# Attention and wave MLP on one core: batches woven in pairs in a fixed order, with x transposed by the DMA crossbar from SBUF to SBUF

## The chip, the cores and the metric

One NeuronCore of a Trainium2 chip. The metric is the time of one execution on the device in microseconds (us); a profile of one execution comes with each kernel. Its span, from the first to the last instruction, is shorter than the time of the same execution: by 1.7 to 2.0 us in every run of which both are on record.

## The reference

Two phases over batch 8, 8 heads, 576 tokens, head size 64 (model width 512). Inputs and output are float32.

```python
# attention in chunks of 64 tokens
scores = q_c @ k_c.T / sqrt(64)            # per head and chunk
x = softmax(scores) @ v_c                  # -> [8, 576, 512]
# wave MLP
theta = x @ w_theta
zr, zi = x * cos(theta), x * sin(theta)
y = w_tok_r @ zr + w_tok_i @ zi            # over the 576 tokens of a batch
u = x + y
out = u + max(u @ w_ch, 0)
```

## The kernel before

It runs attention for all eight batches, keeping x in SBUF, then the MLP for all eight. Tokens lie in five blocks per batch: four of 128 and one of 64. Products are in fp16 with fp32 sums. The MLP, where x has to be transposed for theta and u for the last product:

```python
for b in range(B):
    for sb in range(NSB):                            # five token blocks
        for db in range(NDB):                        # four blocks of 128 channels
            nc.tensor.transpose(pxt[:, db, 0:ns], x16[b][...], id16[0:ns, 0:ns])
        nc.scalar.copy(out=xT[:, :, sb*P : sb*P+ns], in_=pxt[:, :, 0:ns])
    for sb in range(NSB):
        for db in range(NDB):                        # theta: 128 x 512 products
            nc.tensor.matmul(pth[0:ns], xT[:, db, sb*P : sb*P+ns], wtheta16[:, db, :], ...)
        # ScalarE: cos16, sin16;  VectorE: zr16 = x*cos, zi16 = x*sin
    for mt in range(NSB):                            # y: 10 products per block
        ... nc.tensor.matmul(psy[0:nt], wT[0:ns, sb, tsl], z[0:ns, sb, :], ...)
        # VectorE: u16 = psy + x16
    # u16 transposed on TensorE, copied by ScalarE (as x above), then u @ w_ch,
    # VectorE: o32 = max(puw, 0) + u16, and a store on SyncE's queue
    ... (cut)
```

The softmax here doesn't subtract the row's maximum and nothing guards it: scores larger than these inputs give would overflow.

## Time and profile before

| | before |
|---|---|
| time, median of 2 runs | 332.54 us (331.72 to 333.35) |
| span | 329.0 us |
| TensorE busy | 285.2 us, 87% |
| VectorE / ScalarE / GpSimd busy | 44% / 35% / 32% |
| attention, 27 to 127 us | granted clock 0.65 |
| MLP, 127 to 329 us | granted clock 0.97 to 0.99; one batch 24.12 us, all of it TensorE |

The busy shares are averages over two stages with different limits; the lines that show this are in the prediction below. "Granted clock" is the share of TensorE's full clock that the throttle allowed in a stretch.

### The profile page before, as it was taken

To read this page: it belongs to the slowest core of one execution; us is meant where nothing else is said; L and a number is where in the kernel's file an instruction comes from. 1 tells how busy PE (TensorE), PEld (TensorE's weight loads), DVE (VectorE), ACT (ScalarE), POOL (GpSimd) and SP (SyncE) were. 2 spreads that over 40 slices of the span, in tenths; PEclk is the share of its full clock that TensorE was granted. 3 is DMA by queue.
4 is the path that set the end of the run, shared out by engine and by line. 5 is a ranking of instruction groups with operands and counts; after the bars stand their busy time and mean duration, and the time that the engine had idled before them with its cause. 6 is when DMAs were issued, how large, how long until landed. Compare 5 with 4: busy or idle time off the path is not lost.

```text
span 329.0 us, 7260 instructions
## 1 busy us (share of the span) xinstructions
PE 285.2 (87%) x3138; PEld 159.2 (48%) x3138; DVE 146.2 (44%) x319; ACT 115.7 (35%) x290; POOL 105.4 (32%) x132
## 2 busy tenths in 40 slices
PE   0328977879869889999999999999999999999992
PEld 0216866768858777334344344344344344344340
DVE  0216437357347354544534625525535534533532
ACT  0001440431421424805615515425426326227220
POOL 8189999999999900000000000000000000000000
PEclk9999577575676576999999999999999999999998
DMA  6999999999999980003003004004004003003004
GB/s 107 175 134 152 146 138 138 149 142 140 151 138 144 147 44 3 2 0 130 16 0 131 16 0 140 5 0 145 0 0 146 0 0 131 14 1 129 15 1 144
DMA packets 120064, 26.44 MB, mean 80 GB/s; under 512 B 113248, under 2 KB 115424, under 8 KB 120032
## 3 DMA queue, kind: packets, MB, share of 16 engines
q0 software_dynamic: 114784, 16.54, 79.4%
q1 hardware_dynamic: 5248, 9.44, 8.4%
q8 instruction: 24, 0.39, 0.5%
q14 instruction: 8, 0.07, 0.1%
HBM read 33.06 MB, written 9.44 MB: 129 GB/s over the span
## 4 chain that ended last, share of the span: by engine, by line
PE 62%; POOL 14%; DMA 12%; DVE 7%; issue 2%; ACT 1%; DVEq 0%; POOLq 0%; ACTq 0%
PE ps_y L251 30%; POOL qk L107 9%; PE ps_theta L219 8%; PE ps_uw L282 8%; DMA out_dram<-o 5%; POOL v L107 5%; DMA wtok_nat<-in_moe_w_tok_r_dram 3%; PE ps_uT L269 3%; PE ps_sT L142 3%; PE ps_xT L202 2%; PE ps_rs L161 2%; PE ps_wtokT L78 2%; DVE o L290 2%; DMA wtok_nat<-in_moe_w_tok_i_dram 2%; DMA qk<-in_q_dram 2%
## 5 line engine op out<-in xcount | busy, mean ns | idle before, releaser
L251 PE MATMUL ps_y<-zr,wtokTr 128*128 128x512 f16 (+3 forms) x200 | 53.9, 382 | 0.7 <-DVE zr L234 0.6
L251 PE MATMUL ps_y<-zi,wtokTi 128*128 128x512 f16 (+3 forms) x200 | 54.5, 384 | 0.0
L259 DVE TENSOR_TENSOR u<-ps_y,x 128x512 f16<-128x512 f32 (+1 forms) x40 | 27.6, 690 | 53.6 <-PE ps_y L251 53.6
L147 ACT ACTIVATE eT<-ps_sT 128x256 f16<-128x256 f32 x64 | 24.4, 382 | 69.5 <-PE ps_sT L142 66.7
L274 ACT COPY uT<-ps_uT 128x512 f16<-128x512 f16 (+1 forms) x40 | 18.6, 564 | 82.3 <-PE ps_uT L269 82.3
L290 DVE SCALAR_TENSOR_TENSOR o<-ps_uw,u 128x512 f32<-128x512 f32 (+1 forms) x40 | 27.6, 690 | 40.0 <-DMA out_dram<-o 22.5
L107 POOL DMA_DIRECT2D v<-in_v_dram x40 | 37.3, 933 | 1.5 <-DMA wch<-in_moe_w_ch_dram 1.3
L107 POOL DMA_DIRECT2D qk<-in_q_dram x40 | 37.3, 933 | 1.2 <-issue 0.8
L219 PE MATMUL ps_theta<-wtheta,xT 128*128 128x512 f16 (+1 forms) x160 | 36.9, 381 | 0.7 <-ACT xT L207 0.7
L107 POOL DMA_DIRECT2D qk<-in_k_dram x40 | 37.3, 932 | 0.1
L282 PE MATMUL ps_uw<-wch,uT 128*128 128x512 f16 (+1 forms) x160 | 36.9, 381 | 0.0
L251 PEld LDWEIGHTS <-wtokTi 128*128 128x128 f16 (+3 forms) x200 | 16.5, 99 | 38.5 <-issue 29.3
L120 PE MATMUL ps_qkT<-id,qk 128*128 128x128 f16 (+1 forms) x320 | 29.9, 267 | 5.8 <-DMA qk<-in_q_dram 4.5
L142 PE MATMUL ps_sT<-qT,kT 64*64 64x64 f16 x576 | 30.1, 232 | 3.7 <-DVE kT L130 3.6
L251 PEld LDWEIGHTS <-wtokTr 128*128 128x128 f16 (+3 forms) x200 | 17.8, 99 | 31.9 <-issue 17.0
L161 PE MATMUL ps_rs<-ones,eT 64*64 64x1 f16 x576 | 26.9, 191 | 7.0 <-ACT eT L147 7.0
L120 PEld LDWEIGHTS <-qk 128*128 128x128 f16 (+1 forms) x320 | 26.1, 127 | 8.7 <-DMA qk<-in_q_dram 6.1
L230 ACT ACTIVATE sin<-ps_theta,zerob 128x512 f16<-128x512 f32 (+1 forms) x40 | 29.6, 741 | 0.0
L226 ACT ACTIVATE cos<-ps_theta,pihalf 128x512 f16<-128x512 f32 (+1 forms) x40 | 29.5, 737 | 0.0
L207 ACT COPY xT<-ps_xT 128x512 f16<-128x512 f16 (+1 forms) x40 | 18.6, 564 | 28.2 <-PE ps_xT L202 28.2
L161 PEld LDWEIGHTS <-eT 64*64 64x64 f16 x576 | 21.8, 144 | 11.1 <-ACT eT L147 8.9
L185 DVE TENSOR_TENSOR x<-ps_xout,recip 128x512 f16<-128x512 f32 (+1 forms) x40 | 24.6, 681 | 0.4
(39 smaller groups left out, 242.2 us busy)
## 6 DMA issues: line engine op xcount, KB each, us to landing
out_dram<-o SPq DMA_DIRECT2D x32, 256.0 KB, 2.0
qk<-in_q_dram POOLq DMA_DIRECT2D x32, 128.0 KB, 5.5
qk<-in_k_dram POOLq DMA_DIRECT2D x32, 128.0 KB, 5.8
v<-in_v_dram POOLq DMA_DIRECT2D x32, 128.0 KB, 5.8
out_dram<-o SPq DMA_DIRECT2D x8, 128.0 KB, 2.3
wtok_nat<-in_moe_w_tok_r_dram POOLq DMA_DIRECT2D x1, 576.0 KB, 10.0
wtok_nat<-in_moe_w_tok_i_dram POOLq DMA_DIRECT2D x1, 576.0 KB, 6.1
wtheta<-in_moe_w_theta_dram POOLq DMA_DIRECT2D x1, 512.0 KB, 6.1
```

The costliest lines, as they stand in the source:

```text
L107: nc.gpsimd.dma_start(dst, t_ap[b, :, sb * P : sb * P + ns, :].rearrange("h s d -> s h d"),)
L120: nc.tensor.transpose(pqk[:, which, e, 0:ns], qk16[0:ns, sb, which, 2 * e : 2 * e + 2, :].rearrange("s h d -> s (h d)"), id16[0:ns, 0:ns],)
L142: nc.tensor.matmul(pst[cp * CH : cp * CH + CH, cb, :], kT[par * D : par * D + D, e, sl], qT[par * D : par * D + D, e, sl],)
L161: nc.tensor.matmul(ps_rs[cp * CH : cp * CH + CH, cb, h : h + 1], eT[cp * CH : cp * CH + CH, h, cb, :], ones16[cp * CH : cp * CH + CH, :],)
L185: nc.vector.tensor_tensor(out=x16[b][0:ns, sb, :].rearrange("s (h d) -> s h d", h=H), in0=psx[0:ns], in1=recip[0:ns, sb, :].unsqueeze(-1). ...
L219: nc.tensor.matmul(pth[0:ns], xT[:, db, sb * P : sb * P + ns], wtheta16[:, db, :], start=(db == 0), stop=(db == NDB - 1),)
L226: nc.scalar.activation(out=cos16[0:ns, sb, :], in_=pth[0:ns], func=AF.Sin, bias=pihalf[0:ns], scale=1.0,)
L230: nc.scalar.activation(out=sin16[0:ns, sb, :], in_=pth[0:ns], func=AF.Sin, bias=zerob[0:ns], scale=1.0,)
L251: nc.tensor.matmul(psy[0:nt], wT[0:ns, sb, tsl], z[0:ns, sb, :], start=(step == 0), stop=(step == nsteps - 1),)
L259: nc.vector.tensor_tensor(out=u16[0:nt, mt, :], in0=psy[0:nt], in1=x16[b][0:nt, mt, :], op=ALU.add,)
L282: nc.tensor.matmul(puw[0:nt], uT[:, db, mt * P : mt * P + nt], wch16[:, db, :], start=(db == 0), stop=(db == NDB - 1),)
L290: nc.vector.scalar_tensor_tensor(out=o32[0:nt], in0=puw[0:nt], scalar=0.0, in1=u16[0:nt, mt, :], op0=ALU.max, op1=ALU.add,)
```

## The change

The intent: the two stages bind different things, so run them woven. Two batches become one pair of 1152 tokens, nine full tiles of 128 instead of ten blocks. While TensorE does the MLP of pair p, steps of attention of pair p+1 are put between its steps, in an order that the program fixes. y comes out already transposed, row sums come from a column of ones in v, and x is transposed not by TensorE and ScalarE but by a DMA through the crossbar, SBUF to SBUF, issued from SyncE's queue, where the output stores and two small moves of the middle tile stand too. The diff, cut to its core:

```diff
+def weave(main, filler):                 # spread the filler steps evenly over the main steps
+    ...
+    def a1(p, g): ...                    # q, k transposed on TensorE, copied by VectorE
+    def a2(p, g): ...                    # scores, exp
+    def a3(p, j, g): ...                 # numerator and row sum, x tile j (VectorE)
+    def a4(p, g):
+        j0, n = GROUPS[g]                # groups of 2, 2, 1, 2, 2 tiles
+        for j in range(j0, j0 + n):
+            nc.sync.dma_start_transpose(
+                st[p]["xT"][:, :, j * P : j * P + P], st[p]["x"][:, j, :]
+            )
+    def a5(p, g): ...                    # theta from xT, cos, sin, zr, zi
+    def y(p, bb, db): ...                # y transposed: 9 x 2 products of 288 columns
+    def w(p, j): ...                     # u @ w_ch, u back by identity, relu, sum, store (SyncE)
+    def back(p, gs):
+        steps = []
+        for i in range(len(gs) + 2):
+            if i < len(gs):
+                j0, n = GROUPS[gs[i]]
+                steps += [c(a3, p, j, gs[i]) for j in range(j0, j0 + n)]
+            if 0 <= i - 1 < len(gs):
+                steps.append(c(a4, p, gs[i - 1]))     # one group after its x
+            if 0 <= i - 2 < len(gs):
+                steps.append(c(a5, p, gs[i - 2]))     # two groups after its x
+        return steps
+    # pair 0:        weave(y0, rest of its own attention), weave(y1, front(1)), weave(w, back(1))
+    # pairs 1 and 2: weave(y0, front(p+1)), weave(y1 and w, back(p+1))
+    # pair 3:        y0, y1 and w alone
-    for b in range(B): ...               # the attention loop and the MLP loop go
```

## The prediction

> **What bounds the kernel now.** I read the page's slices first, then the windows of its stages, then the chain that ended last in order of time, then the groups of instructions by shape.
>
> ```profile
> PE   0328977879869889999999999999999999999992
> PEclk9999577575676576999999999999999999999998
> DMA  6999999999999980003003004004004003003004
> 27.00:127.20 100.20, 83.68 (x2050) 74.48 (x2050) 51.95 (x136) 30.20 (x128) 87.27 (x105) 0.65 2.25 130
> 152.97:329.00 176.03, 169.12 (x910) 69.60 (x910) 78.05 (x143) 72.47 (x140) 0.00 (x0) 0.99 0.15 51
> ```
>
> Two programs run one after the other. Until 127 us (15 slices) the DMA engines are full and TensorE's granted clock is 0.65 on average: attention of eight batches, 100.2/8 = 12.5 us each, after 27 us in which TensorE hardly works. Then loads are over, the clock is 0.99, TensorE is busy without a gap: the MLP. (Columns of the windows: stretch, length, busy us of PE, weight loads, DVE, ACT, POOL, then clock, DMA share, GB/s.)
>
> ```profile
> 201.15 1.22 PE ps_xT L202 x20
> 202.37 4.54 PE ps_theta L219 x20
> 206.91 12.60 PE ps_y L251 x50
> 219.51 1.22 PE ps_uT L269 x20
> 220.73 4.54 PE ps_uw L282 x20
> ```
>
> This is one batch of the MLP in the chain (start, us, what): nothing but TensorE, 1.22 + 4.54 + 12.60 + 1.22 + 4.54 = 24.12 us, eight times. So in this stage a column taken from TensorE is worth its time, and work of ACT and DVE is free.
>
> ```profile
> 62.27 0.88 POOL v L107
> 63.14 1.37 POOL qk L107 x2
> L180 PE MATMUL ps_xout<-v,eT 64*64 64x64 f16 x576 | 23.3, 238 | 0.0
> L120 PE MATMUL ps_qkT<-id,qk 128*128 128x128 f16 x256 | 25.2, 285 | 0.8 <-DMA qk<-in_k_dram 0.8
> ```
>
> In attention, up to 88 us, the chain is mostly GpSimd issuing q, k and v loads, one per 0.87 us for 128 tokens and 0.67 for 64. The 285 ns of a transpose is its pipelined duration; its spacing is 1.22/20 = 61 ns in the MLP stage and 2.71/32 = 85 ns under the low clock. The 64x64 products come every 1.93/61 = 32 ns.
>
> **What the Trainium skill says.** "TensorE: Matmul & The Clock Gate", Back-to-back issue gap: N/2.4 + 2.5 ns when warm, 216 ns for N = 512. The trace agrees: 20 theta products are 20 x 0.2158 = 4.32 us, and the remaining 0.22 of 4.54 is a bubble at the change to the 64-column group. I use the formula for N = 288: 122.5 ns, an estimate. The same page, The HAM clock gate: activity releases a throttle to half clock; the trace agrees in kind (0.65 among small products, 0.99 among large ones). "VectorE: DVE Perf Modes", The three transpose paths: 1309 ns for a 128x128 DMA crossbar transpose, 390 on TensorE; no run yet shows the first. "Advanced Engine Details and Errata", X-Bar Transpose (TRN2): transposes as fast as regular DMAs. From these I estimate 2 to 4 us from issue to landing of one 128x512 transpose; the 256 KB output stores of this trace land in 2.0.
>
> **The change part by part.** Two batches become one sequence of 1152 tokens, nine full tiles of 128 instead of 2 x (4 full + 1 half). TensorE per pair, at full clock:
>
> - q/k transposes: 9 x 8 = 72 x 61 ns = 4.4 us.
> - Scores: 9 x 16 = 144 x 32 ns = 4.6. Numerator: also 144, 4.6. The row sums (2 x 72 products) go: a column of ones in v gives them (65 columns for 64).
> - x transposes leave TensorE (2 x 1.22 = 2.4 saved) and their ten copies (0.56 us each) leave ACT.
> - theta: 9 x 4 = 36 x 216 ns = 7.8 (before 2 x 4.54 = 9.1).
> - y: 2 x 4 x 9 x 2 = 144 products of 288 columns x 122.5 ns = 17.6 (before 25.2). Fully used K blocks (nine per batch, real and imaginary tails sharing one, instead of ten) and 576 = 2 x 288 columns do this; y comes out transposed, so the u transposes go.
> - w: 36 x (216 + 61) = 10.0, the 61 being the product with the identity that brings u back (before 2 x (4.54 + 1.22) = 11.5).
>
> Sum: 49.0 us per pair. Before, a pair took 2 x (12.5 + 24.1) = 73.2. The new program changes between small and large products some 14 times each way per pair; at half the 0.22 us bubble above per edge that is 3 us, and I allow 2 more for a clock below full where attention is woven in: 54 per pair.
>
> The other engines, per pair, from the durations of before (about 1.1 ns a column for ACT, 0.62 us for 512 fp32 columns and 0.34 for 512 fp16 ones on DVE): ACT exp 5.0, cosine and sine 10.0, relu 5.2, two or three table loads of 1.28, about 23; DVE 5.2 (q/k copies) + 6.5 (x) + 5.4 (z) + 5.6 (u) + 5.6 (out) = 28. Loads: 24 x 0.87 + 6 x 0.67 = 25 us of issuing. All are under 54, so TensorE should bind once started.
>
> The transposes: 36, nine per pair, on SyncE's queue with the stores. In the steady pairs six steps lie between a group's x and its theta, with some four y or w steps among them: 6 to 10 us. The chain x (1.5 us of DVE), issue, landing is some 5 to 6 us: hidden. What they take from TensorE (10 us in all) is gained; in the first pair a few us show.
>
> Start: 18 issues for tiles 0 to 4 end near 17 us, landing near 21.5. Theta and both token weights (3.7 MB at the 290 GB/s that 3.4 MB in 11.5 us show at the start of the trace) land by 34; tiles 5 to 8 by 45; w_ch by 48; pair 1 by 73. The last token-weight transposes and three theta steps (8 us) follow 34, so y of batch 0 starts near 42 and its last block waits for the middle tile's z and its move between partitions, until 46. Then front and back of tiles 5 to 8 (8 us, plus some 4 of waits for exp and the transposes), nine weight transposes (5), three y blocks (6.6): to about 71. Then 17.6/2 + 9 + 3 = 21 for y of batch 1 with the front of pair 1: 92; w and the back of pair 1 (22.4 + 3.5): 118; two pairs of 54: 226; the last pair 27.6 and a tail of 3: 257. The measured time exceeds the span by 332.5 - 329.0 = 3.5: 260 us.
>
> **The rivals.**
>
> 1. The crossbar transposes become the wait. If one holds the queue for 4 us or more, nine take 36 us of a back stretch of about 31, theta waits in TensorE's fixed order, and stores queue behind them. For it: the skill's own 1309 ns against 390; loads of the next pair fill the same engines. Against it: the slack above. This makes +5 to +10 us per pair: 280 to 300; at 10 us each, about 330, nothing gained.
> 2. The clock. If the fronts and the y around them run at 0.65 as attention did, three stretches of 18 us gain up to 8 us each: 280. Against: half of the stretch is dense 288-column products.
> 3. Loads bind. All 33 MB at 290 GB/s are 114 us and now have to arrive within the first 170; the six q/k buffers stop the loading of tiles 6 to 8 until the front of their own pair begins, so each front could wait 2 to 4 us: +10.
> 4. Everything overlaps better than assumed, no edge bubbles and full clock: 49 per pair and less in the first: 240.
>
> **Range and chances.** TensorE's sum alone (4 x 49 + 8 for the token weights) with a start of 34 us is 238, so below 240 is unlikely. Rivals 1 to 3 together, in their moderate forms, reach 288. Only the extreme form of rival 1 gives the gain back. Predicted 260, range 240 to 288; faster 0.94, same 0.03, slower 0.03.
>
> **What would show it.** y: products of 288 columns about 122 ns apart, 17.6 us per pair. In the windows of pairs 1 and 2: TensorE busy above 90%, clock above 0.85, about 54 us each. The transposes' issue-to-landing median: 2 to 4 us confirms hiding; 8 or more, with theta waiting for DMA for over 10 us in total, is rival 1. Front transposes waiting for q or k loads after 80 us is rival 3. Until about 45 us TensorE should wait for loads. I am wrong if steady pairs take over 60 us, or if the first pair ends its y much later than 71 us.

## The result, and the profile after

The changed kernel takes 288.2 us (286.35 to 290.05, 2 runs); its ratio to before is 0.8686 (95% interval 0.8598 to 0.8774). It is a clear gain, and 28 us less of one than predicted: the median lies just outside the range, the faster of the two runs inside it.

The same slices of the page as were shown of before:

```profile
PE   1461975695999852975997968968998999599993
PEclk9999989579799995797798897995999999979998
DMA  9999999999009999946099994344790233620025
```

The two stages are gone; loads now reach to the last quarter. But TensorE has notches, slices with 2 to 7, and the clock has them too. The groups (line, engine, what, count, then busy us, mean ns, and the idle time ahead with what ended it), and the list of waits:

```profile
L254 PE MATMUL ps_theta<-wtheta,xT 128*128 128x512 f16 x144 | 49.5, 495 | 30.9 <-DMA xT<-x 30.0
L305 PE MATMUL ps_y<-wT,zr 128*128 128x288 f16 x288 | 44.8, 296 | 5.8 <-DMA zr<-zmid 5.1
PE ps_theta L254 <- DMA xT<-x: 30.0, 18, 8.0
PE ps_qkT L177 <- DMA qk<-in_q_dram: 10.0, 6, 5.1
```

(In the list of waits the three numbers are us in total, times, and the longest.) Theta waits 30.0 us in 18 places, up to 8.0 us in one, for the crossbar. Its products take 495 ns on average, where they took 381 before. The other waits are smaller and lie mostly in the start.

The stages, with columns as in the prediction's windows: two back stretches and, between them, one front.

```profile
100.00:141.00 41.00, 27.32 (x244) 12.93 (x238) 18.71 (x38) 14.81 (x20) 9.93 (x13) 0.79 1.08 131
141.00:159.00 18.00, 16.44 (x291) 13.00 (x289) 9.49 (x11) 6.52 (x7) 16.27 (x19) 0.94 1.82 116
220.00:256.30 36.30, 30.87 (x311) 16.93 (x309) 21.69 (x41) 13.71 (x18) 0.00 (x0) 0.95 0.37 102
```

The front (141 to 159) is dense and its clock is 0.94. The back stretch at 100 us has TensorE idle for 13.7 of 41 us, at clock 0.79. The one at 220 us, with more work but no loads beside it (GpSimd 0.00), takes 36.3. The chain of waits through the first of them, in order of time (start, us, what):

```profile
102.02 0.69 DVE x L232
102.71 0.60 DVE o L340
...
104.99 0.59 DVE o L340
...
105.71 0.23 SPq L342
...
106.00 7.55 DMA xT<-x
113.59 3.60 PE ps_theta L254 x8
...
121.19 1.74 PE ps_theta L254 x8
...
132.90 0.54 SPq L342
133.44 0.06 issue
133.49 2.44 DMA xT<-x
135.98 3.60 PE ps_theta L254 x8
```

Read it so. The first group's second x tile is written at 102.02 + 0.69 = 102.71; with it the group is complete. Its first transpose goes out only at 106.00: three stores (L342) stand ahead in SyncE's queue, and the last of them waits for its sum on VectorE (L340, done at 105.58). The transpose lands 7.55 us later. Eight theta products follow in 3.60 us, at a granted clock of 0.50; eight others, which did not wait, take 1.74, at 1.00. So this wait costs twice: itself, and the half clock after it. In the whole chain of this profile six such groups of eight, at clocks of 0.50 to 0.56, took 20.9 us together, where 6 x 1.74 = 10.4 would do. Not every wait was followed at once by the low clock: four products after a wait of 3.05 us (at 131.51) still ran at 1.00. At the end of the stretch the last group's transposes stand behind two moves and a store, and land in 2.44 us; by then loads were few.

```profile
L243 SPq DMA_TRANSPOSE xT<-x x36: 1189/1257/2236, 20.9 to 251.7; - x36
DMA to landing us min/median/max: 2.4/2.8/10.6
```

One transpose holds the queue 1257 ns (the median), and lands 2.4 to 10.6 us after issue. Plain stores from the same queue show the same spread: the four issued between 101 and 109 us, beside the loads, landed in 4.8 to 6.6 us, the six between 120 and 133 us, after them, in 2.0 to 2.4. So the slow landing is not the crossbar's alone.

Where the time lies, by stages of the profile. The boundaries are the end of the fifth y block of pair 0 (the first of batch 1) and the first y of each later pair. The prediction's 71 and 47 were for a boundary just before that fifth block; they are moved here by its 2.2 us:

| stage, us | predicted | changed kernel |
|---|---|---|
| start, to the end of the first y block of batch 1 | 73 | 84.1 |
| rest of y of batch 1, front and back of pair 1 | 45 | 55.5 |
| pair 1 with pair 2's attention | 54 | 61.7 |
| pair 2 with pair 3's attention | 54 | 55.0 |
| pair 3 alone, tail | 31 | 32.0 |

### The profile page after: what moved, and what is told of

Same layout as the page of the kernel before. It is cut to its first block, busy times and chain, and to the rows that moved or that the text cites. A ratio compares the mean times of both kernels' runs of the same rounds, so it can differ in the third digit from the quotient of the medians.

```text
span 288.3 us, 5894 instructions
## 1 busy us (share of the span) xinstructions
PE 221.2 (77%) x2548; PEld 139.6 (48%) x2548; DVE 129.9 (45%) x217; ACT 95.2 (33%) x116; POOL 105.6 (37%) x133
## 4 chain that ended last, share of the span: by engine, by line
PE 43%; DMA 25%; POOL 11%; DVE 8%; SPq 5%; issue 4%; ACT 3%; POOLq 0%
PE ps_y L305 18%; DMA xT<-x 13%; PE ps_theta L254 10%; POOL qk L109 8%; PE ps_uw L325 7%; DMA qk<-in_k_dram 6%; DMA wnat<-in_moe_w_tok_r_dram 4%; SPq L243 3%; POOL v L117 3%; PE ps_x L224 2%; DVE o L340 2%; PE ps_qkT L177 2%; DMA zr<-zmid 2%; DVE x L232 2%; PE ps_wT L145 2%
## 5 line engine op out<-in xcount | busy, mean ns | idle before, releaser
L254 PE MATMUL ps_theta<-wtheta,xT 128*128 128x512 f16 x144 | 49.5, 495 | 30.9 <-DMA xT<-x 30.0
L109 POOL DMA_DIRECT2D qk<-in_q_dram x40 | 35.9, 913 | 98.7 <-PE ps_qkT L177 91.5
L305 PE MATMUL ps_y<-wT,zr 128*128 128x288 f16 x288 | 44.8, 296 | 5.8 <-DMA zr<-zmid 5.1
L325 PE MATMUL ps_uw<-wch,uT 128*128 128x512 f16 x144 | 43.2, 387 | 1.2 <-ACT sin L268 0.8
L313 DVE TENSOR_TENSOR uT<-ps_y,xT 128x576 f16<-128x576 f32 x32 | 24.2, 756 | 42.4 <-PE ps_y L305 42.4
L305 PE MATMUL ps_y<-wT,zi 128*128 128x288 f16 x288 | 41.9, 292 | 0.0
L273 DVE TENSOR_TENSOR zr<-x,cos 128x1024 f16<-128x1024 f16 x16 | 11.1, 692 | 64.8 <-ACT cos L264 64.8
L117 POOL DMA_DIRECT2D v<-in_v_dram x40 | 36.3, 911 | 1.4 <-DMA qk<-in_q_dram 1.3
L305 PEld LDWEIGHTS <-zr 128*128 128x128 f16 x288 | 27.5, 101 | 15.9 <-issue 7.7
L177 PE MATMUL ps_qkT<-id,qk 128*128 128x128 f16 x288 | 24.6, 242 | 13.1 <-DMA qk<-in_q_dram 10.0
L305 PEld LDWEIGHTS <-zi 128*128 128x128 f16 x288 | 28.9, 100 | 8.0
L332 PE MATMUL ps_uw<-id,uT 128*128 128x128 f16 x144 | 31.9, 222 | 0.0
L184 DVE COPY qkT<-ps_qkT 128x2048 f16<-128x2048 f16 (+1 forms) x20 | 22.1, 1115 | 20.2 <-PE ps_qkT L177 19.7
L340 DVE TENSOR_TENSOR o<-ps_uw,relu 128x512 f32<-128x512 f32 x36 | 24.6, 687 | 10.8 <-ACT relu L338 10.6
L177 PEld LDWEIGHTS <-qk 128*128 128x128 f16 x288 | 19.8, 108 | 16.9 <-DMA qk<-in_q_dram 11.4
L232 DVE TENSOR_TENSOR x<-ps_x,recip 128x512 f16<-128x512 f32 x36 | 24.9, 691 | 1.2
```

The costliest lines, as they stand in the source:

```text
L109: nc.gpsimd.dma_start(t[pp : pp + n, ti], ap[2 * p + bb, :, s0 : s0 + n, :].rearrange("h s d -> s h d"),)
L117: nc.gpsimd.dma_start(v16[pp : pp + n, slot, :, 0:D], v[2 * p + bb, :, s0 : s0 + n, :].rearrange("h s d -> s h d"),)
L177: nc.tensor.transpose(psv[:, w, e, jj * P : jj * P + P], t[:, w, 2 * e : 2 * e + 2, :].rearrange("s h d -> s (h d)"), id16,)
L184: nc.vector.tensor_copy(out=qkT[:, :, :, 0 : n * P], in_=psv[:, :, :, 0 : n * P])
L232: nc.vector.tensor_tensor(out=st[p]["x"][:, j, :].rearrange("s (f h d) -> s f h d", f=2, h=NE), in0=px[:, :, :, 0:D], in1=recip.broadcast_ ...
L254: nc.tensor.matmul(ps[:, jj * DM : jj * DM + DM], st[p]["xT"][:, db, j * P : j * P + P], wtheta16[:, db, :], start=(db == 0), stop=(db == ...
```

## The experiments

Two theories of why theta waits. **Q**: the transposes go out late, because the program's order puts them one group later, behind stores in a queue that keeps its order. **L**: they land slowly, because loads fill the DMA engines at that time. A rival to both: the missing time is not the crossbar's at all, but the start's loads and the other engines'. The first four kernels ran together on one chip, the next four together, the last three together; the kernel before had medians of 332.69, 331.92 and 331.37 us in these. Profiled runs of e1, e3 and e5 were the slowest of their four (1.5% or more above the fastest), so their spans are only used roughly. One run each of e4, e6 and e11 was slow too. The times given are medians over all runs, the ratios are of fast runs alone. The changed kernel itself ran only twice, earlier, and its interval (0.8598 to 0.8774) is worth about 3 us either way.

### e1_early: transposes one group earlier

```diff
-                steps += [c(a3, p, j, gs[i]) for j in range(j0, j0 + n)]
-            if 0 <= i - 1 < len(gs):
-                steps.append(c(a4, p, gs[i - 1]))
+                steps += [c(a3, p, j, gs[i]) for j in range(j0, j0 + n - 1)]
+                steps.append(<a3 of the group's last tile, then a4 of the group>)
```

> The changed kernel with one edit: the crossbar transposes of a group are issued directly after its last x tile, one group earlier in the fixed order, so ahead of up to three output stores on SyncE's queue. Nothing else moves. Theory Q (the transposes come late because they stand behind stores in one queue that keeps its order): in the first back stretch the first pair of transposes went out at 106.0 us although x was ready at 102.7; they now go out near 103, TensorE's waits for xT fall from 30 us to 15-20, and the time from 288 to 274-280. Theory L (the landing is slow while loads fill the DMA engines: 7.5 us at 106 us, 2.4 us at 251 us when loads were over): the waits fall by no more than 5 us, time 283-288.

Measured: 263.93 us, ratio 0.7918 to before; waits for xT 17.1 us. More gain than theory Q said. But the edit does two things, and e5 and e6 take them apart.

### e2_pe: the crossbar undone

```diff
-        for j in range(j0, j0 + n):
-            nc.sync.dma_start_transpose(xT[:, :, j*P : j*P+P], x[:, j, :])
+        ps = psum2("ps_xT", FP16)
+        for jj in range(n):
+            for db in range(NDB):
+                nc.tensor.transpose(psv[:, db, jj*P : jj*P+P], x[:, j0+jj, db*P : db*P+P], id16)
+        nc.scalar.copy(out=xT[:, :, j0*P : (j0+n)*P], in_=psv[:, :, 0 : n*P])
```

> The changed kernel with the crossbar undone: x is transposed on TensorE into PSUM and copied to xT by ScalarE, at the same places of the same order. It costs 144 transposes x 61 ns = 8.8 us of TensorE and about 5 us of ScalarE per pair. If the waits for the crossbar are the missing time (30 us of waits, and a throttled clock after each of the 8 us ones), the time is 256-266, within 6 us of the 260 predicted; theta's waits are below 5 us in total. Rival (the first pair is bound by loads and the back stretches by ScalarE and VectorE anyway): 275-290, with the waits turned into waits for x on VectorE or for the copies on ScalarE.

Measured: 252.58 us (251.01 to 254.74), ratio 0.7605, clock 0.986. Below the expected range. The work that the change took off TensorE is back on it, and the kernel is 36 us faster. In the list of waits no theta waits for xT; what is left at TensorE is the start's loads and small waits:

```profile
PE ps_qkT L177 <- DMA qk<-in_q_dram: 10.0, 6, 5.2
PE ps_y L313 <- DMA zr<-zmid: 3.7, 1, 3.7
PE ps_theta L262 <- ACT sin L276: 1.8, 1, 1.8
PE ps_xT L246 <- DVE x L232: 1.5, 4, 0.4
```

So the rival, which held that the other engines and the loads would keep the time at 275 to 290, is refuted: the missing time hangs on the crossbar.

### e3_longrows: the same bytes in fewer pieces

```diff
-                    ap[2 * p + bb, :, s0 : s0 + n, :].rearrange("h s d -> s h d"),
+                    <rows of 512 contiguous elements of the same tensor>,     # q and k, wrong on purpose
```

> Wrong result on purpose: q and k are loaded as contiguous rows of 512 elements, the same bytes into the same tiles, but one piece of 2 KB where there were eight of 256 B; v stays as it is. So the DMA engines have 10 pieces per token in place of 24, and everything else is unchanged. Theory L (landing slow under loads): the transposes' slow landings (5.9 to 9.0 us in the first pair, 7.5 at 106 us) shorten to 3-4 us, waits for xT fall from 30 to 10-15 us, time 262-275. Theory Q (queue order): landings shorten little or the issue stays late; waits for xT stay above 20 us, and the time falls only by what the start gains, to 278-285.

Measured: 275.74 us, ratio 0.8282 (its result passed the comparison, whose tolerance doesn't see this mix-up). Waits for xT stayed at 30.0 us in 18 places. In the profile the first transposes of the first full back stretch still took 6.2 us to land (7.55 in the changed kernel), and the slowest 10.5. So the number of pieces of q and k does not make the waits. The 12 us gained lie elsewhere, in the start and in the stretches with pair 1's and pair 2's fronts, each 3 to 4 us shorter. Neither theory had both numbers right; whether it is the bytes or v's pieces that slow the landing is left open.

### e4_stores_act: stores off SyncE's queue

```diff
-            nc.sync.dma_start(out[...], o[pp : pp + n])
+            pending.append((out[...], o[pp : pp + n]))     # issued by nc.scalar.dma_start in the next w step
```

> The changed kernel with the output stores issued from ScalarE's queue, each one step later, so that SyncE's queue holds only the transposes and the two moves of the middle tile. A transpose can then go out as soon as x is written. Theory Q: waits for xT fall to 10-18 us, time 270-278, if ScalarE's 10 extra issues per pair (about 0.55 us each) do not delay it. Theory L: waits stay above 22 us, time 282-290.

Measured: 272.58 us, ratio 0.8178; waits for xT 19.8 us (expected 10 to 18). In pair 1's stretch, the first transpose of pair 2's back now went out 0.1 us after its x, at 154.90 for an x done at 154.82. But landing was late: the second tile's x was done at 157.01, and theta had its transpose only at 165.16; GpSimd was issuing loads in that time. The median from issue to landing rose from 2.8 to 6.0 us. So taking stores out of the way is worth 16 us, and early transposes meet the loads instead. Both theories have a part.

### e5_late14 and e6_early19: which half of e1

In e1 the transposes also stopped counting as steps of the weave, so the back had 14 steps to spread and not 19. e5 does only that; e6 only issues early:

```diff
 # e5: a4 stays after the next group's last x, but shares that step
-                steps.append(c(a4, p, gs[i - 1]))
+                steps.append(<the preceding step, then a4 of group i - 1>)
 # e6: a4 directly after its own group's x, still a step
+                steps.append(c(a4, p, gs[i]))         # in the place of the later one
```

> e1_early changed two things at once: the transposes go out one group earlier, and they no longer count as a step of the weave, so 14 steps of the back, not 19, are spread over the y and w steps and each group's theta comes later in the order. Here only the second: the transposes stay one group later, right after the next group's last x, but are not counted. If the spacing made most of e1's 24 us, this is 266-274; if the place in SyncE's queue did, 279-287.

> The other half of e1_early: the transposes are issued directly after their group's last x, but stay a counted step, so the spacing of TensorE's work is nearly that of the changed kernel. If the place in the queue made most of e1's gain, 266-274; if the spacing did, 279-287. The waits for xT should be between the 30 us of the changed kernel and the 17 of e1 in either case.

| | 19 steps | 14 steps |
|---|---|---|
| transposes one group later | 288.2 (the change) | 289.72 (e5) |
| transposes directly after x | 264.01 (e6) | 263.93 (e1) |

The spacing is worth nothing that these runs can tell; the earlier place is worth all 24 us. e6's waits for xT are 11.1 us in 7 places. SyncE's queue in e6, in the stretch where the changed kernel's first transposes went out at 106.00:

```profile
99.72 2.62 SPq L342 DMA_DIRECT2D out_dram<-o  x2
102.39 3.03 SPq L243 DMA_TRANSPOSE xT<-x  x2
105.52 0.52 SPq L342 DMA_DIRECT2D out_dram<-o  x1
106.09 2.76 SPq L243 DMA_TRANSPOSE xT<-x  x2
```

e6's second x tile is done at 101.38, so the first transpose is out 1.0 us later and not 3.3: two stores stand ahead of it, not three. At the end of a stretch the last transposes no longer stand behind the middle tile's moves. (In e6 the moves come last instead, and cost a wait of 0.4 us there once.)

### e7_noloads: loads taken away after the first pair

```diff
     def load_qk(p, j):
+        if p > 0:
+            nats[p, j] = keep        # one tile of q and k that stays; v of pair 0 is used again
+            return
```

> Wrong result on purpose: after the first pair no q, k or v is loaded; pairs 1 to 3 take one tile of q and k that stays, and pair 0's v. Two small loads are added at the start. Everything else is the changed kernel. Theory L (loads in flight make the landing slow): in the back stretches of pairs 1 and 2 the transposes land in about 2.5 us as they do in that of pair 3, these two stretches shrink from 41 and 43 us to 33-36 and 36-38, time 265-274. Theory Q (the queue alone): these stretches shrink by less than 3 us each, time 280-287.

Measured: 268.47 us (wrong result), ratio 0.8106. The stretch that held the 8.0 us wait, from its chain:

```profile
98.66 0.23 SPq L348
98.95 1.22 SPq L249
100.22 2.47 DMA xT<-x
102.74 1.89 PE ps_theta L260 x4
...
120.54 2.43 DMA xT<-x
123.01 3.46 PE ps_theta L260 x8
```

The order is unchanged, and the transposes still go out late, behind stores. But they land in 2.5 us, and so they do in every later stretch. The stages are 77.7, 48.8, 54.5, 54.4 and 32.0 us: pair 1 lost 7 us and now equals pair 2, which never had loads beside its back. So the 20 us are what the later pairs' loads cost, most of it beside the transposes. Waits for xT are still 22.5 us in 19 places, but none is over 3.0; that rest is theory Q's part. Two reserves: without loads the fronts wait for none either (in the changed kernel 1.3 us after 80 us), and 6.4 us of the gain lie in the start, where pair 0's own loads still run; how much of those is the transposes' was not separated. Why loads stand beside the backs: GpSimd waited 91.5 us in 4 places for q and k buffers that the transposes of a front set free, so the next loads begin in the front and run on into the back. Whether more buffers would move them was not tried.

### e10_early_noloads: both together

The edits of e6 and e7.

> Wrong result on purpose: e7's missing loads together with e6's early issue. If the two delays (late issue, slow landing) add up along one chain, each stretch falls to the 47.5 us of e8's last full one or a little below, and only the start keeps its waits: 77.7 + 42 + 47.5 + 47.5 + 32 = 247 of span, time 245-252; waits for xT at TensorE under 8 us, nearly all before 80 us. If early issue alone had already hidden the landing, it would be no better than e6's 264 by more than 5 us.

Measured: 248.71 us (wrong result), ratio 0.7503; waits for xT 5.8 us. Its stages are 79.4, 39.0, 50.0, 48.2 and 32.0. Early issue takes 24.2 us, no loads 19.7, both 39.5: nearly the sum of 43.9. That fits two delays in one chain, from x to theta. Steady pairs came 0.7 to 2.5 us above the 47.5 expected.

### e8_hybrid, e9_hybrid2 and e11_pe_again: a version that beats both?

```diff
     def a4(p, g):
+        if p == 0:        # e9: p < 2
+            <transposes on TensorE, copy on ScalarE, as e2>
+            return
         for j in range(j0, j0 + n):
             nc.sync.dma_start_transpose(...)      # in the order of e1
```

> A version meant to be fast: pair 0, whose back runs while its own and the next pair's loads fill the DMA engines, is transposed on TensorE and ScalarE as in e2_pe; pairs 1 to 3 by the crossbar in the order of e1_early. By the stages of e2 (start 75 us, first full stretch 42) and e1 (48 us a steady pair, 32 the last): span 75 + 42 to 48 + 50 + 48 + 32 = 247 to 253, time 249-256. Below e2's 252.6 only if the crossbar is really free in the steady pairs; 257 or more would mean that it is not.

> Pairs 0 and 1 transposed on TensorE, pairs 2 and 3 by the crossbar in the early order. e8 lost in the first full stretch (47.4 us against e2's 42.1), where the crossbar worked beside loads; that stretch is now TensorE's. From the stages: 75.3 (e2) + 42.1 (e2) + 50.5 (e8) + 47.5 (e8) + 32 = 247.4 us of span, 1 to 2 us below e2; time 249-252, 0.99-1.0 of e11.

> The same program as e2_pe, on the chip of this call, to compare e9_hybrid2 with: 250-255.

Measured: e8 255.08 us (ratio 0.7688), e9 249.59 (0.7527, interval 0.7497 to 0.7557), e11 250.72 (0.7575, interval 0.7543 to 0.7607). By stages:

| us | start | first full | pair 1 | pair 2 | last |
|---|---|---|---|---|---|
| change | 84.1 | 55.5 | 61.7 | 55.0 | 32.0 |
| e6: crossbar, early | 82.1 | 46.9 | 51.5 | 48.6 | 32.0 |
| e2: TensorE | 75.3 | 42.0 | 50.1 | 50.0 | 31.7 |
| e8: TensorE in pair 0 | 75.5 | 47.4 | 50.5 | 47.5 | 32.1 |

Where loads run beside the back (the first two columns) TensorE's transposes win by 5 to 7 us. Where they do not (pair 2) the early crossbar wins, by 1.4 us in e6 and 2.5 in e8, which is about what 36 transposes of 61 ns cost; e9's 48.7 against e11's 49.8 says the same. In pair 1's stretch, with loads beside part of the back, neither is clearly ahead: e6 51.5, e8 50.5 and e9 48.6 with the crossbar, e2 and e11 50.1 without. The mix of both, e9, cannot be told from e11: the intervals overlap. Plain e2, in woven order with TensorE's transposes, is the version to take: 0.76 of before, and simpler.

## Why the prediction was wrong, point by point

The direction, the bound and most terms held; one step failed, and a smaller error in the other direction, by luck, hid part of it.

- **TensorE's work per product: right.** y took 2.21 us for 18 products of 288 columns, 122.8 ns each against the estimated 122.5; eight theta products in a row took 1.74 us, 217.5 each for 216. In e2, with nothing waiting for the crossbar, steady pairs took 50.0 and 50.1 us: 49.0, plus 2.2 of transposes, less 1.2. So the allowance of 5 us per pair for edges and clock was too large: with it and those transposes the prediction's own sum would be 56.
- **"The chain x (1.5 us of DVE), issue, landing is some 5 to 6 us: hidden": the step that failed.** In the first full stretch the chain from the group's second x tile being done to its first xT tile was 113.55 - 102.71 = 10.8 us: 3.3 behind stores, and 7.55 from issue to landing. (The second transpose went out 1.3 us after the first and landed at 114.43, in time for its products.) The slack was also smaller there: theta's turn came at 113.59 - 8.00 = 105.59, only 2.9 us after x. In pair 1's stretch x was done at 164.41, the transposes out at 168.53, theta's turn at 170.50 and its start at 174.38: slack 6.1 us, inside the "6 to 10", chain 9.9. The prediction named stores in the same queue, and the loads, but only as a rival; in the chain that it summed it put no time for the first and the landing of an idle DMA system for the second.
- **Sizes of the two parts: shown, within some 3 us.** The place in the queue 24.2 us (e6), the later pairs' loads 19.7 (e7), both 39.5 (e10). These are differences to the changed kernel. It was run at another time. e5 took 289.72.
- **The crossbar as a gain of 10 us: wrong in sign.** Against TensorE's transposes in the same order it costs 288.2 - 252.6 = 35.6 us.
- **The start, "to about 71": measured 81.7**, the end of the last weight transposes. Of the 11 us, some 9 are the crossbar's (e2: 73.0). In e2 the middle tile's move and loads still show a few us of waiting.
- **Rival 1, "+5 to +10 us per pair: 280 to 300"**, was the one whose total came true, and it named the reason in part. The excess was not even, though: 11, 11, 8, 1 and 1 us by the stages of the table. And the reason was not a transpose of 4 us that fills the queue (1.26 us each), but their place in the queue and their landing.
- **Rival 2, the clock in the fronts: wrong place.** In the 18 us windows of the three fronts (82 to 100, 141 to 159, 202 to 220) the clock was 1.00, 0.94 and 1.00. It fell mostly in the backs, after the waits, where eight theta products took 3.3 to 3.6 us for 1.74.
- **Rival 3, loads bind: small** after the start; y of batch 1 with the front of pair 1 took 16.7 us (81.7 to 98.4), where 21 had been allowed.
- **What would show it:** y, the transposes' median of 2.8 us ("2 to 4 confirms hiding") and theta's waits of over 10 us were all named as signs. The median said "hidden" and the total of waits said "not". The median of 36 hides the ten that land in 6.7 to 10.6 us, and says nothing of the time before issue.
- **Small slips that decided nothing.** The terms of the start add up to 69.6, not 71. VectorE's 0.62 and 0.34 us per 512 columns stand against 0.69 and 0.42 in the trace of before. And 3.5 us were added from span to time, where the same execution shows 1.75.

## What to carry to other kernels

A DMA that stands between two steps of compute has to be judged from the moment its input is ready: time behind other entries of its queue, plus landing beside whatever else moves then, against the work that stands between in program order. Put such a transfer in the queue directly after its producer, ahead of anything that waits for a later result. Moving the transposes off TensorE could free only about 2 us of it per pair, while each exposed wait cost itself and, after many of them, half the clock for the next eight products.

## What the Trainium skill lacked or had wrong

- "VectorE: DVE Perf Modes", The three transpose paths, gives 1309 ns for a 128x128 crossbar transpose. Here a 128x512 one held its queue for 1.26 us and landed in 2.4 to 10.6 us, by what else the DMA engines did (2.5 in all later stretches without loads, e7); the page has neither figure.
- "Advanced Engine Details and Errata", X-Bar Transpose (TRN2), has transposes as fast as regular DMAs. The runs agree as long as nothing else moves: a 128 KB transpose landed in 2.4 to 2.5 us, a 128 KB store in 2.3 at the median. Beside loads the transposes between 106 and 111 us took 7.1 to 7.9, and stores between 101 and 109 us 4.8 to 6.6; the section gives no figure for that case.
- "VectorE: DVE Perf Modes", Rules for kernel authors, says to transpose 128x128 on TensorE if a PSUM destination is OK. The runs agree for the whole kernel (252.6 against 288.2 us), even with TensorE as the bound. But in pair 2's stretch, without loads beside it, crossbar transposes issued early were 1.4 to 2.5 us better (e6, e8); the rule names no such case.
- "DMA: Bandwidth & Descriptors", Rules for kernel authors, advises to issue a DMA early and wait on it late. The runs agree, and give the size: one group earlier was worth 24 us of 288. It does not say that an output store in the same queue, still waiting for its data, holds back a transfer whose data are ready; here that was 3.3 us for one group.
